# Lightweight convolution into a SiLU feed-forward layer: the third block's halo columns are copied by ScalarE instead of Pool

## The chip, the core and the metric

One NeuronCore of a Trainium2 chip runs the whole kernel. The metric is the device time of one execution in microseconds (us). The engines are named as in the profile: PE is TensorE's matmul, PEld its weight load, DVE is VectorE, ACT is ScalarE, POOL is GpSimd, and SP is SyncE, which only issues DMAs here. An engine works through its own queue in order; semaphores tie the queues together.

## What is computed

```python
w = softmax(weight, axis=-1)                    # (8 heads, 7 taps)
x_pad = concat([zeros(B, 6, D), x], axis=1)     # x is (8, 4096, 192), causal padding
out = einsum('hk,bskhg->bshg', w, windows of 7 of x_pad)   # depthwise, taps shared in a head
h = out.reshape(32768, 192) @ w_in              # (192, 2048)
y = (h / (1 + exp(-h))) @ w_out                 # SiLU, then (2048, 192)
```

Everything is float32 in and out. Row t of a sequence needs rows t-6 to t: each block of rows needs the last six rows of the block before it, its halo.

## The kernel before

The 32768 rows are worked in 32 blocks of `TT` = 1024 rows, numbered b = 0 to 31; four blocks make a sequence. The third block is b = 2. On chip a block lies transposed: channels on partitions, rows along the free axis, in two halves of 512 rows, the first on partitions 0 to 63 and the second on 64 to 127. The one tile `xt` holds this for the current block, with `pad` = 6 halo columns in front of the 512 in each of three channel groups k.

Making a block ready takes these steps, one block ahead of its matmuls:

- `load` brings rows from HBM into `nat` (L140), and `turn_in` transposes them on DVE into `xt` (L425).
- `halo_in` fills the halo columns. For the first half they come from a small tile, `tail`: the line L442 copies them on Pool, 64 partitions by 18 elements. For a block that starts a sequence, L440 writes zeros in their place. For the second half a DMA on SP takes them from the first half's last columns (L443). Then `tail_of` saves the block's own last six columns by a DMA into the next `tail` (L435).
- `conv` computes the seven taps: for b of 2 or more the first tap is a multiply on DVE (L454) and the others a multiply-add on DVE (L457). For b below 2 the first tap is on ScalarE (L452). The first tap reads the halo columns, so it waits for all of `halo_in`.
- `spread` copies the result into `dup` by DMAs on SP (L474), and `win` makes sums and differences of these on DVE (L491, L494).

The matmuls of a block follow a scheme with fewer products than the plain one. `product` (L579) and `plain` (L591) write PSUM; for each group, ScalarE copies a partial sum out of PSUM into a tile `u` (L615), DVE adds it to another partial sum (L611), and ScalarE applies SiLU (L627, L632). `out_slot` (L683) is the second layer, `merge` and `turn_out` bring its result together, and `store_out` (L772) writes it out by DMAs on SP.

The scheme needs weights that are combined beforehand. `combine` and `combine_out` do that on Pool, once, by some ninety additions and subtractions (L319, all through the helper `comb`), while the first block is worked in the plain way. The first block's second layer is `down_plain` (L702), which ends in three copies on ScalarE (L715).

From the second block on, the string `PLAN` gives the order: it lists tokens, and `step` turns each into instructions for block b, the block before it or the block after it. `ha.0` in the pass of block b is `halo_in(b + 1)`; so the third block's halo is filled in the pass of the second block, b = 1, which is also the first pass that runs by `PLAN`. In this pass, `ha.0` stands ahead of the first ScalarE token, `u5.0`.

Most instructions of PE, DVE and ScalarE are pinned (`pin`, and the wrappers `vec` and `act`): they keep the order in which the code issues them. The additions of `comb` and the copy L442 go straight to `nc.gpsimd` and are not pinned; the framework's scheduler places them in Pool's queue. In the built program, the copy for b = 2 stands second to last of this queue's preparatory work: the last addition of `combine_out` follows it.

Of the kernel before, what the change touches and what calls it, by code (L numbers as in the profile page):

```python
# [17 lines left out]
def kernel(  # L18
# [24 lines left out]
    nc = tc.nc  # L43
# [7 lines left out]
    R = 64  # L51
    NK = D // R
    grp = D // H
    pad = K - 1
# [60 lines left out]
    def pin(ins):  # L115
        return tc.keep_in_program_order(ins)
# [303 lines left out]
    tails = {}  # L420
# [11 lines left out]
    def tail_of(b):  # L432
        if (b + 1) * TT % S:
            tails[b + 1] = xpool.tile([R, NK, pad], F32, tag="tail", name="tail", bufs=2)
            nc.sync.dma_start(out=tails[b + 1], in_=xts[b][R:P, :, TB : TB + pad])  # L435

    def halo_in(b, _):
        xt = xts[b]
        if b * TT % S == 0:
            nc.gpsimd.memset(xt[0:R, :, 0:pad], 0.0)  # L440
        else:
            nc.gpsimd.tensor_copy(xt[0:R, :, 0:pad], tails.pop(b))  # L442
        nc.sync.dma_start(out=xt[R:P, :, 0:pad], in_=xt[0:R, :, TB : TB + pad])  # L443
        tail_of(b)

# [344 lines left out]
    def step(b, token):  # L790
# [13 lines left out]
        if name[0] == "P":  # L804
            product(b, digits[0], int(name[1:]))
        elif name == "L":
            plain(b, *digits)
        elif name == "SL":
            silu_plain(b, *digits)
        elif name[0] in "uXabS":  # L810
            sums_h(b, name, digits[0])
        elif name == "t":
            sum_g(b, *digits)
        elif name[0] == "D":
            i, (j, e) = int(name[1]), digits
            for half in range(2) if i == 3 and b == NB - 1 else (None,):
                out_slot(b, j, i, e, half)
        elif name[0] in "Mzyx":
            merge(b, name, *digits)
        elif name == "o":  # L820
            turn_out(b, *digits)
        elif name == "st":
            store_out(b, *digits)
        elif name == "ld":
            if b + 1 < NB:
                load(b + 1, digits)
        elif b + 1 < NB:
            {"i": turn_in, "ha": halo_in, "v": conv, "sp": spread, "w": win}[name](
                b + 1, *digits[: 1 + (name == "v")]
            )  # L830
# [212 lines left out]
```

## Time and profile before

| | us |
|---|---|
| median of 4 runs | 2418.73 |
| lowest to highest | 2418.28 to 2419.95 |
| profiled execution, its own time | 2418.76 |
| its span, first to last instruction | 2417.0 |
| PE busy | 2389.7 (99% of the span) |
| DVE busy | 2137.3 (88%) |
| ACT busy | 1149.1 (48%) |
| POOL busy | 115.3 (5%) |

The span leaves out 1.76 us around the first and last instruction. A line such as `ACT u L615 <- PE ps L579` in the view of waits says that ACT, about to write tile u at line 615, waited for PE's write of ps at line 579; the figures are the total, the number of waits and the longest. A line of the timeline has the start, the time taken (from the first start to the last end where several are merged), engine, line, operation, tiles, count, and in brackets the idle time before it with what ended that.

### The profile page before, as it was taken

The page shows a single profiled execution, that of the slowest core. Times are in us where ns is not written, and L with a number is a line of the kernel's source. Part 1 is how long each engine was busy: PE and PEld are TensorE (multiplying, and loading weights), DVE is VectorE, ACT ScalarE, POOL GpSimd, SP SyncE. Part 2 cuts the span into 40 slices and gives each one's busy share as a digit, 9 for nine tenths or more (in the row PEclk, how much of TensorE's full clock was granted, in tenths as well). Part 3 has the DMA queues.
Part 4 walks back from the last instruction along what each step waited for, and adds up shares of the span by engine and source line. Part 5 has one row for each costly group of instructions (what it writes and reads, how often), then busy time and mean ns, then how long its engine had stood idle before and what let it go on. Part 6 is the DMA issues. An engine that isn't in the chain of part 4 may idle for free.

```text
span 2417.0 us, 43592 instructions
## 1 busy us (share of the span) xinstructions
PE 2389.7 (99%) x17630; PEld 979.1 (41%) x17630; DVE 2137.3 (88%) x2967; ACT 1149.1 (48%) x2183; POOL 115.3 (5%) x169
## 2 busy tenths in 40 slices
PE   9789999999999999999999999999999999999998
PEld 4234443444433444434444334443344443344433
DVE  8689888999889898889998899988899988999876
ACT  4145444455444554444554445544445544455443
POOL 5900000000000000000000000000000000000000
PEclk9999999999999999999999999999999999999999
DMA  7411222221222212222212222122222122221111
GB/s 150 80 38 24 42 45 45 51 43 27 47 41 48 51 24 43 44 44 51 45 27 45 41 48 51 26 41 46 42 51 47 25 45 42 48 51 29 26 33 18
DMA packets 451242, 106.54 MB, mean 44 GB/s; under 512 B 423584, under 2 KB 428704, under 8 KB 451040
## 3 DMA queue, kind: packets, MB, share of 16 engines
q1 hardware_dynamic: 447392, 101.78, 23.1%
q8 instruction: 138, 2.26, 0.4%
q0 software_dynamic: 448, 1.58, 0.3%
q10 hardware_dynamic: 3200, 0.39, 0.1%
q14 instruction: 64, 0.52, 0.1%
HBM read 31.46 MB, written 25.17 MB: 23 GB/s over the span
## 4 chain that ended last, share of the span: by engine, by line
PE 94%; DVE 0%; ACT 0%; issue 0%; POOL 0%; ACTq 0%
PE ps L683 47%; PE ps L579 45%; PE ps L591 2%; DVE t L123 0%; DVE nat L457 0%; DVE cmb L123 0%; ACT u L123 0%; DVE g L611 0%; DVE nat L454 0%; DVE osb L123 0%; DVE ps L611 0%; DVE u L611 0%; ACT u L615 0%; POOL wo L319 0%; ACTq L871 0%
## 5 line engine op out<-in xcount | busy, mean ns | idle before, releaser
L579 PE MATMUL ps<-win,ws 64*128 64x512 f32 x1550 | 703.0, 609 | 18.5 <-DVE ps L611 17.8
L683 PE MATMUL ps<-g,wo 128*32 128x512 f32 x2976 | 708.7, 594 | 0.0
L579 PE MATMUL ps<-win,wr 64*128 64x512 f32 x1550 | 656.8, 609 | 0.7 <-ACT u L615 0.7
L615 ACT COPY u<-ps 128x512 f32<-128x512 f32 x775 | 451.1, 587 | 210.6 <-PE ps L579 196.6
L683 PE MATMUL ps<-t,wo 128*32 128x512 f32 (+2 forms) x4528 | 543.6, 446 | 0.0
L683 PE MATMUL ps<-t,wx 128*32 128x512 f32 x2976 | 491.7, 594 | 0.1
L627 ACT ACTIVATE g<-g 128x512 f32<-128x512 f32 x465 | 279.1, 628 | 438.7 <-DVE g L611 438.7
L457 DVE SCALAR_TENSOR_TENSOR nat<-xt,taps,nat 128x512 f32<-128x512 f32 x564 | 419.3, 748 | 7.8 <-ACT nat L452 3.8
L579 PE MATMUL ps<-dup,wr 64*128 64x512 f32 x868 | 411.1, 593 | 0.0
L123 DVE TENSOR_TENSOR t<-g 128x1024 f32<-128x1024 f32 x248 | 301.7, 1217 | 54.6 <-PE ps L683 53.7
L579 PE MATMUL ps<-dup,ws 64*128 64x512 f32 x682 | 345.8, 603 | 0.0
L123 DVE TENSOR_TENSOR t<-g,t 128x1024 f32<-128x1024 f32 x248 | 302.3, 1220 | 46.0 <-PE ps L683 44.9
L579 PEld LDWEIGHTS ps<-win,wr 64*128 64x128 f32 x1550 | 234.5, 186 | 234.1 <-issue 86.2
L611 DVE TENSOR_TENSOR g<-u,ps 128x512 f32<-128x512 f32 x465 | 313.7, 679 | 15.0 <-PE ps L579 14.2
L579 PEld LDWEIGHTS ps<-win,ws 64*128 64x128 f32 x1550 | 240.1, 186 | 177.9 <-DVE ps L611 69.0
L627 ACT ACTIVATE g<-ps 128x512 f32<-128x512 f32 x465 | 263.8, 596 | 56.5 <-PE ps L579 56.5
L683 PEld LDWEIGHTS ps<-t,wo 128*32 128x32 f32 x4528 | 179.1, 110 | 239.4 <-issue 228.6
L611 DVE TENSOR_TENSOR ps<-u,ps 128x512 f32<-128x512 f32 x310 | 214.3, 691 | 58.9 <-ACT u L615 26.3
L683 PE MATMUL ps<-g,wx 128*32 128x512 f32 x1488 | 246.8, 595 | 0.0
L683 PEld LDWEIGHTS ps<-t,wx 128*32 128x32 f32 x2976 | 115.5, 110 | 269.4 <-issue 261.0
L683 PEld LDWEIGHTS ps<-g,wo 128*32 128x32 f32 x2976 | 162.0, 110 | 135.4 <-issue 135.4
L742 ACT COPY cmb<-ps 96x512 f32<-96x512 f32 x30 | 17.5, 582 | 418.8 <-PE ps L683 418.8
(89 smaller groups left out, 1825.9 us busy)
## 6 DMA issues: line engine op xcount, KB each, us to landing
dup<-nat SPq DMA_DIRECT2D x345, 128.0 KB, 2.3
nat<-in_x_dram SPq DMA_DIRECT2D x382, 64.0 KB, 2.5
out_dram<-osb SPq DMA_DIRECT2D x376, 64.0 KB, 2.0
raw<-in_moe_w_out_dram SPq DMA_DIRECT2D x8, 384.0 KB, 4.1
raw<-in_moe_w_in_dram SPq DMA_DIRECT2D x12, 192.0 KB, 4.7
ws<-wr POOLq DMA_DIRECT2D x8, 192.0 KB, 3.5
raw<-in_moe_w_in_dram SPq DMA_DIRECT2D x6, 128.0 KB, 3.1
xt<-xt SPq DMA_DIRECT2D x31, 4.5 KB, 1.9
```

Of the source, the lines that this page charges most:

```text
L123: return lambda *args, **kw: pin(getattr(self.engine, name)(*args, **kw))
L457: nc.vector.scalar_tensor_tensor(out=dst, in0=src, scalar=tap, in1=dst, op0=ALU.mult, op1=ALU.add)
L579: nc.tensor.matmul(to, raw(g, *LEFT[e][r], e), rhs, start=first, stop=True, skip_group_check=True)
L591: nc.tensor.matmul(banks[PLAIN_BANKS[n and 1 + e]][:, cols], rows(wr[j] if own == e else ws[j], e)[:, a, k, :], rows(dups[b], e)[:, SLOT[e ...
L611: pin(nc.vector.tensor_tensor(out_, u, v, op=op))
L615: pin(nc.scalar.copy(us[b, g, o], t1))
L627: pin(nc.scalar.activation(h, src, AF.Silu))
L683: nc.tensor.matmul(accs[b][at][SQ * q : SQ * q + SQ, to], lhs[:, e, SQ * k : SQ * k + SQ], rhs[:, e, ts(q, TB // 4) if i == 5 else to], st ...
L742: pin(nc.scalar.copy(c[0], acc[0][0:n, :]))
```

## The change

For b = 2, and for that block alone, the copy of the halo columns goes to ScalarE and is pinned at the place where the code issues it. All other blocks keep the copy on Pool.

```diff
         if b * TT % S == 0:
             nc.gpsimd.memset(xt[0:R, :, 0:pad], 0.0)
         else:
-            nc.gpsimd.tensor_copy(xt[0:R, :, 0:pad], tails.pop(b))
+            head = xt[0:R, :, 0:pad]
+            if b == 2:
+                pin(nc.scalar.copy(head, tails.pop(b)))
+            else:
+                nc.gpsimd.tensor_copy(head, tails.pop(b))
         nc.sync.dma_start(out=xt[R:P, :, 0:pad], in_=xt[0:R, :, TB : TB + pad])
         tail_of(b)
```

In the built program ScalarE's queue has the new copy right behind the three copies of L715 and ahead of the first copy of L615. Pool's queue lacks it. The orders of PE, DVE and SP are the same as before. The waits of the new copy are those of the old one: the last multiply-add of block b = 1 on DVE, the DMA that filled `tail`, and ScalarE's own first taps of block b = 1.

## The prediction

> **What bounds the kernel now.** I began with the chain that ended last, by engine, and then asked for the waits of PE, because a chain that lies almost wholly on one engine can only shorten where that engine stood idle.
>
> ```profile
> PE 94%; DVE 0%; ACT 0%; issue 0%; POOL 0%; ACTq 0%
> ```
>
> ```profile
> engine line waited for: us in total, times, longest us
> PE ps L579 <- DVE ps L611: 17.8, 1, 17.8
> PE ps L579 <- ACT u L615: 0.7, 1, 0.7
> PE ps L579 <- POOL wr L319: 0.6, 1, 0.6
> ```
>
> The kernel runs at PE's pace and PE waits once in earnest, 17.8 us, for a DVE sum. The blocks behind it follow each other on PE without idle time. So the question is what held that one DVE sum. The timeline of DVE around it:
>
> ```profile
> 107.55 1.84 DVE L425 STREAM_TRANSPOSE xt<-nat 128x512 f32<-128x512 f32 x3
> 122.18 1.19 DVE L454 TENSOR_SCALAR nat<-xt,taps 128x512 f32<-128x512 f32 x2 [12.78 <-POOL xt L442]
> 123.40 2.99 DVE L457 SCALAR_TENSOR_TENSOR nat<-xt,taps,nat 128x512 f32<-128x512 f32 x4
> 126.30 0.69 DVE L611 TENSOR_TENSOR ps<-u,ps 128x512 f32<-128x512 f32 x1
> ```
>
> DVE works in order. The sum at 126.30 stands behind two first taps and four multiply-adds of the third block, and the first of these stood 12.78 us for the halo copy on Pool. The timeline of Pool says why the copy was late:
>
> ```profile
> 119.66 0.59 POOL L319 TENSOR_TENSOR wx<-wx,wo 128x192 f32<-128x192 f32 x1
> 120.33 0.59 POOL L319 TENSOR_TENSOR wx<-wo,wx 128x192 f32<-128x192 f32 x1
> 120.87 1.14 POOL L319 TENSOR_TENSOR wo<-wo 128x192 f32<-128x192 f32 x2
> 121.95 0.19 POOL L442 COPY xt<-tail 64x18 f32<-64x18 f32 x1
> 122.10 0.58 POOL L319 TENSOR_TENSOR wo<-wo 128x192 f32<-128x192 f32 x1
> ```
>
> Pool had no gap: the copy waited for no data, only for its turn behind the weight additions. The path to the stall is Pool's queue, then copy, taps, sum, and PE at 127.05.
>
> **What the change removes.** The copy leaves Pool's queue. Its conditions were met long before: the last multiply-add of block b = 1 ended at 97.88 (a run of 18 that starts at 81.75 and takes 16.13), and the DMA into `tail` was issued at 80.0, with 1.9 us to landing. ScalarE comes to it here:
>
> ```profile
> 102.07 0.59 ACT L715 COPY cmb<-ps 128x512 f32<-128x512 f32 x1 [0.27 <-PE ps L702]
> 103.11 0.59 ACT L615 COPY u<-ps 128x512 f32<-128x512 f32 x1 [0.46 <-PE ps L579]
> ```
>
> The last L715 copy ends at 102.66, and that is when the new copy can start. Its price on ScalarE has no row of its own. The nearest are ScalarE's 32x128 copies (L734, 256 ns mean) and the 128x1 activation at the start (203 ns); I take 0.25. It fits into the 0.46 us in which ScalarE waits for PE. If it did not, the `u` copies behind it would move, PE waits for those at 103.75, and each microsecond would cost one there; but PE then still runs into the stall, so up to several microseconds stay covered by it. Cost: nothing. Two table loads of 1.28 us, should the copy need them, would lie under the same cover.
>
> The Trainium skill, "TensorE: Matmul & The Clock Gate", in the section on the array's architectural detail, states that ScalarE's queue is strict first in, first out, so a waiting copy there would hold up every `u` copy and SiLU behind it. By that rule alone the move would be a danger; here nothing of its waits is left at 102.66, so it adds nothing to the sum.
>
> **What is late next.** DVE's first tap needs three things: the halo copy (now about 102.9), DVE's own transposes (ended 109.39), and the DMA L443 for the second half's halo, on SP:
>
> ```profile
> 106.46 6.34 SPq L772 DMA_DIRECT2D out_dram<-osb  x12
> 112.91 0.64 SPq L443 DMA_DIRECT2D xt<-xt  x1
> ```
>
> It stands behind the twelve stores of the first block, is issued at 112.91 and takes 1.9 us from issue to landing (the row of DMA issues for this stretch). Nothing ahead of it on SP depends on the copy, so it lands at 114.8, and the taps start at about 114.85 in place of 122.18: 7.33 us earlier. The new limit is this DMA, not the copy.
>
> **What the earlier start runs into.** From 109.4 to 122 DVE stood still and Pool had its inputs to itself. With taps from 114.85, both work. The trace shows what that costs on both sides: the 18 multiply-adds at 81.75, beside Pool, went at (16.13 - 1.0) / 17 = 0.89 us each, the four at 123.40, without it, at (126.30 - 123.40) / 4 = 0.725. And the two first taps:
>
> ```profile
> L454 DVE TENSOR_SCALAR nat<-xt,taps x2: 474/633/792, 122.2 to 122.9; 128x512 f32<-128x512 f32 x2
> ```
>
> The first, beside Pool's last addition, took 0.79 us and the second 0.47; from start to start the slow one held DVE for 0.72 and the fast one for 0.50. So before the sum: one more slow tap, 0.22, and four slow multiply-adds, 4 x (0.89 - 0.725) = 0.66; together 0.88 us. The sum itself reads PSUM and has no row beside Pool in this place; I leave it. It starts at 114.85 + (126.30 - 122.18) + 0.88 = 119.85, and PE follows 0.75 later, as before: 120.60 in place of 127.05. Gain 6.45 us. Without contention it would be 7.33; with all six instructions and the sum at the worst row's ratio, 0.79 / 0.47 = 1.68 times, 4.12 + 0.69 becomes 8.1 and the gain 4.1.
>
> Pool pays too: its additions take 0.45 alone and 0.79 beside DVE (64x128), so the 7.6 us of work left at 114.85 could last 7.6 x 0.79 / 0.45 = 13.3 us, to 128.2. What it makes then is weights. The first-layer ones are finished two microseconds after 114.85 before and, slowed, at about 118.2, ahead of PE's restart; the last ones are for L683, which PE starts 25 us after the restart (152.15 against 127.05). Cover is ample; if it were gone, each late microsecond would be one of PE's.
>
> **The clock.** PE stands still for 11.4 us (109.23 to 120.60) in place of 17.8. The granted clock in this stretch, by windows:
>
> ```profile
> 109.40:127.00 17.60, 0.00 (x0) 0.00 (x0) 4.72 (x8) 0.58 (x2) 12.20 (x26) 0.60 0.28 42
> 127.00:130.00 3.00, 2.96 (x10) 1.75 (x12) 2.24 (x4) 0.59 (x1) 0.00 (x0) 0.51 0.00 0
> 130.00:140.00 10.00, 10.00 (x52) 5.14 (x52) 6.83 (x12) 5.92 (x12) 0.00 (x0) 1.00 0.01 2
> ```
>
> The clock is the figure after POOL's. A mean of 0.60 over 17.6 us is 3.5 us at full and the rest at half speed, so it fell near 112.9, and it came back near 129.95, 2.9 us after the restart; those 2.9 us at half speed cost PE 1.45. With 11.4 us idle it still falls, so I take the same cost again, a difference of nothing. No row shows another restart; I bound it by -1.45 (back at once) and +1.45 (twice as long). The four runs, 1.67 us apart, leave room for that.
>
> The same page of the skill, Part 1, says that the clock is set by free-running windows of 3.4 us, so the slow stretch after a restart depends on where in a window it falls. By that rule an estimate of the stretch is anything up to two windows, 6.8 us, which costs at most (6.8 - 2.9) / 2 = 1.95 us more than before and 1.45 less at best; the trace's 2.9 agrees with it but shows one case.
>
> **The sum.** Behind the restart the work is the same and PE has no idle time in which the shift could be lost. The profiled execution's own time of 2418.76 becomes 2418.76 - 6.45 = 2412.3. The median, 2418.73, is 0.03 lower, so the same.
>
> **The rivals.**
> (a) As worked out, 2412.3; with the bounds on contention at none and on the clock at half their width, 2410.9 to 2413.8. Chance 0.83.
> (b) The halo DMA is late. It has become the limit, and its lines show landings from 1.8 up to 3.7 us. At 3.7 the gain is 6.45 - 1.8 = 4.65, and with 0.3 lost to the clock 4.35: 2414.4. For it: stores and loads share its queue. Against it: this very DMA took 1.9 in the same surroundings. Chance 0.10. The heavy contention above gives about the same time.
> (c) Nothing moves, because DVE was really held by something else that ended at 122.1: 2418.7. Pool's copy ended at 122.14 and DVE began at 122.18, and nothing else in sight ended there. Chance 0.04.
> (d) Slower: the copy holds up ScalarE's queue. Behind it stand three `u` copies that the DVE sum needs, 4.2 us from the first's start (103.11) to the third's end (107.32), and then 0.75 to PE. PE restarts later than before only if the copy ends after 127.05 - 0.75 - 4.2 = 122.1; from there each microsecond costs one. An end at 128 gives 2424.7. Against it are the conditions met by 97.88, 24 us of margin. Chance 0.03.
>
> **How the numbers follow.** A difference under 0.2%, 4.8 us, is about what a measurement of this kernel can't tell from none. Case (a) is faster throughout; of (b) the half with landings up to 3.5 us reaches 4.8. So faster has 0.83 + 0.05 = 0.88, same 0.05 + 0.04 = 0.09, slower 0.03. The range takes (a) and (b): 2410.9 to 2414.4.
>
> **What would show it.** In the changed profile: a ScalarE copy of 64x18 near 102.7; DVE's first tap near 114.9, held by the DMA L443's landing; multiply-adds of 0.8 to 0.9 us until Pool ends at 126 to 128; PE's one wait at about 11.4 us; and, from there on, each block 6 to 7 us earlier. I am wrong if the first tap starts later than 117, if PE waits for Pool's weights after the restart, or if a new idle stretch opens later on PE.

## The result, and the profile after

| | us |
|---|---|
| before, median of 60 runs | 2419.49 (2416.82 to 2422.24) |
| after, median of 40 runs | 2415.11 (2412.71 to 2416.55) |
| after against before, ratio | 0.9982, 95% interval 0.9978 to 0.9987 |
| forecast | 2412.3, range 2410.9 to 2414.4 |

The change makes the kernel faster by 4.4 us, 0.18%. The direction is as forecast, the size is not: 6.45 us were forecast, and the time lies above the range. The first four runs of before had a median 0.76 us lower than the sixty, so part of the miss is the base; the larger part is the gain.

The profiled execution has a span of 2414.2 us, against 2417.0. The lines of `kernel.py` behind the edit stand four further down: L442 is now L444 for the third block, L454 is L458, L457 is L461, L579 is L583, L611 (the sum on DVE) is L615, L615 (the `u` copy on ScalarE) is L619. The chain that ended last and the waits of PE, after:

```profile
PE 94%; DVE 3%; SPq 1%; DMA 1%; issue 0%; ACT 0%; ACTq 0%; DVEq 0%
```

```profile
engine line waited for: us in total, times, longest us
PE ps L583 <- DVE ps L615: 12.9, 1, 12.9
```

The one long wait is still there and still for the same sum; it went from 17.8 to 12.9 us, where 11.4 were forecast. ScalarE's queue shows the copy (start, time taken, then what it is):

```profile
102.10 0.20 ACT L444 COPY xt<-tail 64x18 f32<-64x18 f32 x1
102.66 0.59 ACT L619 COPY u<-ps 128x512 f32<-128x512 f32 x1 [0.35 <-PE ps L583]
```

It takes 0.20 us, and the `u` copy behind it still waits for PE. Then SP's queue and DVE's:

```profile
113.60 0.63 SPq L447 DMA_DIRECT2D xt<-xt  x1
```

```profile
108.25 1.85 DVE L425 STREAM_TRANSPOSE xt<-nat 128x512 f32<-128x512 f32 x3
115.60 1.24 DVE L458 TENSOR_SCALAR nat<-xt,taps 128x512 f32<-128x512 f32 x2 [5.51 <-DMA xt<-xt]
116.88 5.32 DVE L461 SCALAR_TENSOR_TENSOR nat<-xt,taps,nat 128x512 f32<-128x512 f32 x4
122.11 0.68 DVE L615 TENSOR_TENSOR ps<-u,ps 128x512 f32<-128x512 f32 x1
```

The first taps now wait for the halo DMA, as forecast. But the four multiply-adds take 5.32 us, where the kernel before needed 2.99 and 3.6 were forecast. One of them alone, from the rows of L461 in this stretch (shortest, median and longest in ns):

```profile
L461 DVE SCALAR_TENSOR_TENSOR nat<-xt,taps,nat x1: 2464/2464/2464, 117.7 to 117.7; 128x512 f32<-128x512 f32 x1
```

And what Pool did meanwhile (the profile before has 114 such additions and subtractions on Pool in all):

```profile
117.23 0.78 POOL L319 TENSOR_TENSOR ws<-wr,ws 64x128 f32<-64x128 f32 x1
117.97 0.58 POOL L319 TENSOR_TENSOR wx<-wo 128x192 f32<-128x192 f32 x1
118.52 0.58 POOL L319 TENSOR_TENSOR wo<-wo 128x192 f32<-128x192 f32 x1
119.06 0.58 POOL L319 TENSOR_TENSOR wx<-wx,wo 128x192 f32<-128x192 f32 x1
119.72 0.92 POOL L319 TENSOR_TENSOR wx<-wo,wx 128x192 f32<-128x192 f32 x1
```

Three additions follow each other every 0.55 us at the 0.58 us that Pool needs with DVE still. 3 x 0.55 = 1.64, and 2.464 - 0.823 (the shortest multiply-add in this stretch) = 1.64: the times are those of a multiply-add that did not advance during these three. The other five multiply-adds of the stretch took 0.82 to 1.14 us, and most of Pool's 128x192 additions beside them 0.92 to 1.04: there both were slowed and both went on. The last view is the clock, by windows (the figure after POOL's):

```profile
110.00:122.80 12.80, 0.00 (x0) 0.00 (x0) 7.19 (x9) 0.66 (x2) 11.72 (x22) 0.69 0.39 59
122.80:128.60 5.80, 5.75 (x20) 3.57 (x22) 3.20 (x4) 0.97 (x2) 3.06 (x4) 0.51 0.01 3
128.60:140.00 11.40, 11.40 (x54) 5.49 (x50) 8.32 (x13) 7.98 (x15) 0.00 (x0) 1.00 0.00 1
```

PE restarted at 122.85. A mean of 0.51 over the second window puts the return to full speed near 128.45, so PE ran at half speed for 5.6 us, against 2.9 before: 1.35 us more lost than in the first profile.

### The profile page after: what moved, and what is told of

Read it like the earlier page. It is cut to its first block, busy times and chain, and to the rows that moved or that the text cites. A ratio compares the mean times of both kernels' runs of the same rounds, so it can differ in the third digit from the quotient of the medians.

```text
span 2414.2 us, 43590 instructions
## 1 busy us (share of the span) xinstructions
PE 2390.9 (99%) x17630; PEld 982.8 (41%) x17630; DVE 2140.4 (89%) x2967; ACT 1149.1 (48%) x2184; POOL 116.4 (5%) x168
## 4 chain that ended last, share of the span: by engine, by line
PE 94%; DVE 3%; SPq 1%; DMA 1%; issue 0%; ACT 0%; ACTq 0%; DVEq 0%
PE ps L687 47%; PE ps L583 45%; PE ps L595 2%; DVE two L123 1%; DVE nat L461 1%; DVE mh L123 0%; SPq L140 0%; SPq L776 0%; DMA nat<-in_x_dram 0%; DMA raw<-in_moe_w_in_dram 0%; DMA xt<-xt 0%; SPq L235 0%; DVE win L495 0%; SPq L230 0%; DMA dup<-nat 0%
## 5 line engine op out<-in xcount | busy, mean ns | idle before, releaser
L583 PE MATMUL ps<-win,ws 64*128 64x512 f32 x1550 | 703.5, 610 | 13.6 <-DVE ps L615 12.9
L583 PE MATMUL ps<-win,wr 64*128 64x512 f32 x1550 | 656.7, 609 | 0.7 <-ACT u L619 0.7
L619 ACT COPY u<-ps 128x512 f32<-128x512 f32 x775 | 451.1, 587 | 207.4 <-PE ps L583 191.2
L461 DVE SCALAR_TENSOR_TENSOR nat<-xt,taps,nat 128x512 f32<-128x512 f32 x564 | 422.2, 753 | 7.8 <-ACT nat L456 3.8
L583 PE MATMUL ps<-dup,wr 64*128 64x512 f32 x868 | 411.7, 594 | 0.8 <-POOL wr L319 0.8
L583 PE MATMUL ps<-dup,ws 64*128 64x512 f32 x682 | 345.8, 603 | 0.0
L583 PEld LDWEIGHTS ps<-win,wr 64*128 64x128 f32 x1550 | 234.7, 186 | 234.5 <-issue 86.8
L615 DVE TENSOR_TENSOR g<-u,ps 128x512 f32<-128x512 f32 x465 | 313.7, 679 | 15.1 <-PE ps L583 14.2
L583 PEld LDWEIGHTS ps<-win,ws 64*128 64x128 f32 x1550 | 240.3, 186 | 173.1 <-DVE ps L615 64.1
L615 DVE TENSOR_TENSOR ps<-u,ps 128x512 f32<-128x512 f32 x310 | 214.3, 691 | 58.3 <-ACT u L619 26.3
```

The source lines that it names most:

```text
L461: nc.vector.scalar_tensor_tensor(out=dst, in0=src, scalar=tap, in1=dst, op0=ALU.mult, op1=ALU.add)
L583: nc.tensor.matmul(to, raw(g, *LEFT[e][r], e), rhs, start=first, stop=True, skip_group_check=True)
L615: pin(nc.vector.tensor_tensor(out_, u, v, op=op))
L619: pin(nc.scalar.copy(us[b, g, o], t1))
```

## The experiments

Theory A: the missing gain was lost to Pool, which shut DVE out. Theory B: something else slowed DVE. Theory C: the clock took it. Each run is set against the kernel before on the same chip, which had medians of 2419.3 to 2419.5 us.

**The changed kernel again** (no edit).

> The changed kernel once more, unaltered, for a second profile. Known: 2415.1 us against 2419.5 before; in its first profile the four multiply-adds ahead of the sum took 5.2 us, one of them 2.46, where 3.6 were forecast. Theory A (Pool's unpaused additions of 128x192 shut DVE out of its inputs): it comes again, one of the four takes about 1.6 us more than 0.82, and PE's wait is 12 to 13 us. Theory B (a chance of that one execution): no multiply-add over 1.1 us, the four take 3.6, and PE's wait is 11.4.

Measured: 2414.51 us, ratio 0.9978 (0.9970 to 0.9987).

```profile
115.11 1.25 DVE L458 TENSOR_SCALAR nat<-xt,taps 128x512 f32<-128x512 f32 x2 [5.50 <-DMA xt<-xt]
116.40 5.31 DVE L461 SCALAR_TENSOR_TENSOR nat<-xt,taps,nat 128x512 f32<-128x512 f32 x4
121.63 0.68 DVE L615 TENSOR_TENSOR ps<-u,ps 128x512 f32<-128x512 f32 x1
```

The 5.3 us come again, with a longest multiply-add of 2464 ns once more. It is no chance of one execution: the same three additions meet a multiply-add again.

**Additions held back**, with the copy on ScalarE (`late`) and, with the same edit, on Pool (`late_before`):

```diff
+        def comb(out, u, v, op):
+            pool.tensor_tensor(out, u, v, op=op)
...
-        if (b, token) == (1, "ha.0"):
+        if (b, token) == (1, "v.12"):
             assert not any(t[0] == "D" for c, t in did if c == 1)
+            pool.tensor_copy(wx[0][:, 0, 0, 0:1], nats[2][:, 1, 0, 0:1])
             for j in range(NJ):
                 combine_out(j)
```

The first lines stand in `combine_out`; `pool` is the pinned wrapper of Pool. The one-column copy reads what the last tap ahead of the sum has written, so the additions behind it wait for this tap.

> The changed kernel, with the additions of combine_out held back on Pool until the last tap ahead of the sum is done (a one-column copy on Pool reads this tap's result, and the additions stand behind it). Theory A (contention with Pool is what the gain lost): the six taps before the sum take 4.1 us as in the kernel before, the sum starts at about 119.7 and PE's wait falls from 12.9 to about 10.5; 2412.7 us, 2.4 less than the changed kernel. Theory B (DVE was slowed by something else, the loads and stores of that stretch or ScalarE): the taps still take 6.5, PE's wait stays near 12.9, 2415.1.

> The kernel before, halo copy on Pool, with the same additions held back. Theory A (the copy was late only for its place in Pool's queue behind these additions, and the halo DMA of the second half is the next limit): the copy comes before 114, the first tap waits for the DMA at about 115, and the time is that of the run with the copy on ScalarE and the additions held back, 2412.7 within 0.7. Rival (the move to ScalarE matters in itself): it stays clearly above that, up to 2419.5.

Measured: `late` 2411.86 us, ratio 0.9967 (0.9954 to 0.9979); `late_before` 2411.28, ratio 0.9965 (0.9953 to 0.9978). DVE in `late`:

```profile
115.52 0.88 DVE L461 TENSOR_SCALAR nat<-xt,taps 128x512 f32<-128x512 f32 x2 [6.43 <-DMA xt<-xt]
116.44 2.99 DVE L464 SCALAR_TENSOR_TENSOR nat<-xt,taps,nat 128x512 f32<-128x512 f32 x4
119.34 0.69 DVE L618 TENSOR_TENSOR ps<-u,ps 128x512 f32<-128x512 f32 x1
```

With Pool still, the four take 2.99 again and the sum comes 3.82 us after the first tap, in place of 6.51. The loads and stores still run in this stretch (the issue of the twelve stores even took 7.26 us in place of 6.34), so theory B falls. Holding the additions back is worth 2414.51 - 2411.86 = 2.65 us, close to the 2.7 by which the taps became shorter; all five runs of `late` lie below all forty of the changed kernel. Both times came out below the 2412.7 expected. PE's wait was 12.3, not the 10.5 expected, though it restarted at 120.1: it had also come to the wait earlier. Pool and the first tap in `late_before`:

```profile
112.55 0.19 POOL L445 COPY xt<-tail 64x18 f32<-64x18 f32 x1
118.84 0.18 POOL L123 COPY wx<-nat 128x1 f32<-128x1 f32 x1 [6.09 <-DVE nat L460]
```

```profile
114.87 0.88 DVE L457 TENSOR_SCALAR nat<-xt,taps 128x512 f32<-128x512 f32 x2 [5.50 <-DMA xt<-xt]
```

The copy on Pool is in time as soon as the additions no longer stand ahead of it, and the DMA is the limit there too. So it was the place in the queue, not the engine: with the additions held back, the kernel gains 8.3 us with the copy on Pool and 7.7 with it on ScalarE, against 5.0 for the changed kernel on the same chip. Part of this gain is the contention that the same edit takes away.

**Additions in the code's order** (`inorder`): the changed kernel with the additions of `combine_out` pinned as above, but neither held back nor moved to another token.

> The changed kernel with the additions of combine_out pinned on Pool in the order of the code, but not held back: all sixteen then run after the last addition of combine, and nearly each waits for the one ahead of it. Theory A1 (DVE is shut out whole only while Pool runs several additions without a pause, 1.6 us for the three in the changed kernel): no tap takes more than 1.4 us, the six taps take 5.0 to 5.5, the sum starts near 120.5, 2413.5. Theory A2 (any 128x192 additions shut DVE out, whatever their order): the taps take 6.5 or more and the time is 2415 or above.

Measured: 2413.14 us, ratio 0.9973 (0.9962 to 0.9983). The multiply-adds of the stretch:

```profile
L464 DVE SCALAR_TENSOR_TENSOR nat<-xt,taps,nat x6: 958/961/1073, 116.3 to 121.8; 128x512 f32<-128x512 f32 x6
```

Pool's 128x192 additions run beside all of them, and none is shut out: 0.96 to 1.07 us each. The first tap to the sum takes 5.18 us, inside the 5.0 to 5.5 of A1, so A2 falls. But A1, that a run of additions without a pause shuts DVE out, does not follow. Pool's rows here:

```profile
116.09 0.65 POOL L123 TENSOR_TENSOR wx<-wo,wx 128x192 f32<-128x192 f32 x1
116.70 1.03 POOL L123 TENSOR_TENSOR wo<-wo 128x192 f32<-128x192 f32 x1
117.69 1.03 POOL L123 TENSOR_TENSOR wx<-wo 128x192 f32<-128x192 f32 x1
```

These three follow each other without a pause too, and both engines went on. The order of the additions decides whether the standstill comes; what in the order does it is not shown.

**PE kept busy through the stall** (`heat`):

```diff
+        if (b, token) == (1, "P1.0"):
+            for _ in range(12):
+                pin(
+                    nc.tensor.matmul(
+                        banks[6],
+                        zeros,
+                        zeros.unsqueeze(1).to_broadcast([P, 4, P]),
+                        start=True,
+                        stop=True,
+                        skip_group_check=True,
+                    )
+                )
         if name[0] == "P":
             product(b, digits[0], int(name[1:]))
```

> The changed kernel, with 12 idle matmuls of 128x512 on zeros in front of the product that waits for the sum, into a bank that nothing else uses then. By the products' rate they take about 10.3 of the 12.9 us. Theory C (part of the loss is the clock, at half speed for 2.9 us after the restart before and 5.7 in the profile after): the granted clock stays at 1.00, the restart is at full speed, and the time falls by 1.4 to 2.9 us, to about 2412.9, with less spread. Rival (the clock's share is only in the profiled execution): 2415.1.

Measured: 2413.13 us, ratio 0.9972 (0.9961 to 0.9983), 1.4 less than the changed kernel beside it. But it is no clean test: PE still waited 2.6 us at the end, and the clock did not stay up as expected: it fell at 123.0, just after the restart at 122.46, and was low for 3.4 us. The taps, too, met Pool differently: one first tap took 1.81 us, beside the same three additions at 0.58 us each, a second case of the standstill. PE restarted as late as in the second profile of the changed kernel (122.37), where the slow stretch lasted 6.0 us; (6.0 - 3.4) / 2 = 1.3 us fits the 1.4. So the clock costs something, of the order of a microsecond; one profile does not measure how much.

**The kernel before again** (`before_again`, no edit).

> The kernel before once more, unaltered, for a second profile: how long the clock stays at half speed after PE's restart. If the 2.9 us of the first profile were short by chance, this one shows more, like the 4.7 to 6.1 us of the runs so far; if a longer stall makes a shorter slow stretch, it shows about 2.9 again. PE's wait 17.8, 2419.5 us within 1.5.

Measured: one time, 2419.07 us; PE's wait 17.8 again. The windows of the first profile, here:

```profile
127.00:130.00 3.00, 2.84 (x10) 1.64 (x12) 2.25 (x5) 0.58 (x1) 0.00 (x0) 0.50 0.00 0
130.00:140.00 10.00, 10.00 (x48) 5.29 (x46) 5.76 (x10) 4.73 (x10) 0.00 (x0) 0.89 0.01 2
```

A mean of 0.89 over 10 us is 2.2 us at half speed: the clock came back near 132.2, 5.1 us after the restart at 127.16. The 2.9 us that the forecast was built on were at the short end. The clock by windows of 0.1 us and, from the chain, the start of the first long stretch of second-layer matmuls, in two profiles of each kernel:

| | before | before again | after | after again |
|---|---|---|---|---|
| clock falls | 112.89 | 111.76 | 114.79 | 111.34 |
| PE restarts | 127.05 | 127.16 | 122.85 | 122.37 |
| clock is back | 129.96 | 132.24 | 128.45 | 128.40 |
| half speed after the restart | 2.9 | 5.1 | 5.6 | 6.0 |
| second layer starts | 164.17 | 165.35 | 161.31 | 161.04 |

Against `before_again`, where the slow stretch is nearly as long, the changed kernel is 4.0 and 4.3 us ahead, close to the 4.4 of the medians, and its PE restarts 4.3 and 4.8 us earlier. So the clock explains why the first pair of profiles is only 2.8 us apart. That it takes nothing from the medians is likely, but two profiles of each kernel do not show it.

From fall to return the clock was at half speed for 17.07, 20.48, 13.66 and 17.06 us: 5, 6, 4 and 5 steps of 3.41, to 0.02 us. A restart paid the rest of the step into which it fell and, in three of the four, the next one whole; where the steps lie differs between executions of one program.

**Halo ahead of the stores** (`early_lb`, on top of `late_before`): `turn_out` and `store_out` of the first block are issued at `ha.0`, behind `halo_in`.

```diff
+        if (b, token) == (1, "ha.0"):
+            out_first()
...
-    for k in range(NK):
-        turn_out(0, k)
-        store_out(0, k)
+    def out_first():
+        for k in range(NK):
+            turn_out(0, k)
+            store_out(0, k)
```

> The kernel before with the additions held back and the first block's output transposes and stores issued behind the third block's halo. Theory (the halo DMA behind the twelve stores is the limit once the copy is early): DVE transposes the third block at about 105.7, the DMA is issued near 108 and lands near 110, the taps start at 110 to 110.5 or, if Pool's copy comes at 112.5, at 112.7; PE's wait falls from 11.7 to 7 to 9.5; 2407 to 2409.5 us. Rival (something else holds DVE): 2411.3 as without the move.

Measured: 2410.14 us, ratio 0.9961 (0.9948 to 0.9973), a little above the expected range.

```profile
107.51 0.63 SPq L446 DMA_DIRECT2D xt<-xt  x1
```

```profile
112.66 0.88 DVE L457 TENSOR_SCALAR nat<-xt,taps 128x512 f32<-128x512 f32 x2 [3.44 <-POOL xt L445]
```

The DMA goes out 5.4 us earlier than in `late_before`, and the limit is Pool's copy again, which stands behind the additions of `combine`. PE restarts at 117.23 in place of 119.43, but its slow stretch lasted 5.8 us here, against 5.3.

**Sums ahead of the taps** (`spread`, then `spread_a`, and `spread_b` with the copy on Pool):

```diff
+    put_off = []
     for b in range(1, NB + 2):
-        for s in plan:
+        for n, s in enumerate(plan):
             for t in s:
-                step(b, t)
+                if b == 1 and t[:2] == "v." and (n < 53 or put_off):
+                    put_off.append(t)
+                else:
+                    step(b, t)
+            if put_off and n > 52 and n % 3 == 2:
+                step(b, put_off.pop(0))
```

The first of the three lacked `(n < 53 or put_off)`. In it the last tap of a channel group comes behind the DMAs that spread the group's result, so it leaves this tap out of what the matmuls read and does not compute the layer; it serves for its time alone.

> The changed kernel, where the third block's taps are put behind the first four sums and then given one by one to every third slot of the plan in this pass. Theory (PE's stall is nothing but the taps standing ahead of the sums in DVE's queue): PE's long wait is gone, at most 3 us are left at that place, and the time falls by up to 11 us under the changed kernel, to 2404; what DVE then has too much in the rest of the pass can give back some us as short waits of PE, so 2404 to 2409. Rival (DVE lacks the time in this pass, and PE waits as long, only later): 2413 to 2417.

> The changed kernel with the taps put behind the sums as in the run before this one, where the last tap of a channel group came behind the DMAs that spread it; here it comes ahead of them again. Theory (PE's stall was the order of taps and sums in DVE's queue, and DVE has the time for the taps later in the pass): 2404.3 within 0.8, no wait of PE over 1 us behind 104. Rival (the earlier run was that fast for its misplaced tap): above 2406.

> The same order of taps and sums with the halo copy on Pool, as in the kernel before. Theory (the copy stays behind Pool's additions until about 122, and the first tap, which DVE reaches at about 116, waits for it): DVE stands for some 5 to 6 us at the first tap, PE for 4 to 6, and the time is 2408 to 2410; the move to ScalarE is then worth 4 to 6 us in this order too. Rival (the sums ahead of the taps leave enough slack to hide the late copy): 2404 to 2405, and the copy's place no longer matters.

Measured: `spread` 2404.35 us, ratio 0.9934 (0.9922 to 0.9947); `spread_a` 2404.65, ratio 0.9937 (0.9925 to 0.9950); `spread_b` 2410.06, ratio 0.9960 (0.9946 to 0.9973). PE's longest wait for DVE in `spread_a`, and DVE's wait for Pool in `spread_b`:

```profile
PE ps L583 <- DVE ps L615: 2.6, 1, 2.6
```

```profile
DVE nat L454 <- POOL xt L442: 6.1, 1, 6.1
```

The sums depend on nothing that the taps make. Issued first, they free PE at 110.4, the clock is at half speed for 3.4 us only (111.1 to 114.5), and DVE finds time for the taps later. `spread_a` beats both kernels, by 14.6 us over before; its one wait of 2.6 us was expected under 1. In `spread_b` the late copy costs 2410.06 - 2404.65 = 5.4 us: in this order too, getting it out from behind the additions is needed.

## Why the prediction was right, and where not

- **The stall and its chain** (Pool's queue, copy, taps, sum, PE): right. `late_before` and `spread_a` each break it at another link, and PE's wait follows. The blocks behind it came 2.9 to 4.3 us earlier, by the profiles compared, where 6 to 7 were forecast.
- **The copy on ScalarE**: right, 0.20 us at 102.10, forecast 0.25 near 102.7. It moved nothing.
- **The halo DMA as next limit**: right. Its landing took 1.9 us again. The first tap started at 115.60 and 115.11 in place of 114.85, because DVE's work ahead of it, and with it the DMA's issue, lay 0.7 and 0.2 us later in these executions.
- **"What the earlier start runs into"**: the step that failed, by its size. Contention was named as the price of the earlier start, but charged by the mean of 18 multiply-adds beside other additions, 0.88 us in all. From the first tap to the sum 6.51 and 6.52 us passed, against 5.0 forecast and 4.12 before: contention cost 2.4, of which 1.64 is one multiply-add that stood still for three additions. The rate came from a stretch whose 18 multiply-adds took at most 1.08 us each, and was carried to one in which Pool's additions come in another order. The 2.4 in place of 0.88 is 1.5 us of the 2.1 by which the gain fell short (6.45 against 4.4). The later first tap, named above, took another 0.75 and 0.26 us in the two profiles; the two together leave 4.2 and 4.7 us of the 6.45, which is how much earlier PE restarted in them than in the first profile before. `late` puts the contention at 2.65 us of time.
- **The range** does not follow from its sentence: contention at none and half the clock's width give 2410.7 to 2413.0, while 2410.9 and 2413.8 are 2412.3 with the clock's full 1.45 on either side. And it left out what the text itself had worked out: the heavy bound on contention, a gain of 4.1, gives 2414.7, above the range's end. The measured 4.4 lies close to it. Rival (b), a late DMA, came to a similar time for a wrong reason.
- **The clock**: "the same cost again" fits the medians, and is wrong between the first two profiles, since 2.9 us was a short sample. The bound of +1.45 was about met: 1.35 in one profile of the changed kernel, 1.55 in the other. The Trainium skill ("TensorE: Matmul & The Clock Gate", Part 1) states a free-running window of about 3.4 us. The steps of 3.41 us in these profiles agree with it, and the estimate of up to two windows, 6.8 us, covers the 2.9 to 6.0 seen after the restart; it would have been the better guide to the spread.
- **Pool's lateness**: right. Its additions ended at 125.9 and 125.4 (126 to 128 forecast), and PE waited for none of them after the restart.
- **The chance of 0.88** for faster by over 0.2%, 4.8 us, stood on this step above all: with contention at its measured price the forecast gain is 7.33 - 2.39 = 4.9, on that line, and the measured 4.4 lies below it. That a change under 0.2% can't be told from none was wrong: the interval of the ratio is 0.0005 to either side.

## What to carry to other kernels

When a wait goes, ask what now runs at the same time that ran in turns before, and price that overlap by the worst row as well as by the mean. Here the bound by the worst row, a gain of 4.1 us, lay next to the measured 4.4, though no row of the profile before showed a standstill. A helper's late result can be a matter of the queue it stands in, as here: look first at the order ahead of it, and at what is queued behind the waiter without needing it, before moving work to another engine. Here the order of two groups on DVE alone gained 9.2 us (`spread_b`), about twice the move; both together gained 14.6.

## What the runs showed of the hardware

Pool and DVE slow each other unevenly. A 128x512 multiply-add took 0.75 us alone, 0.82 to 1.14 beside most additions, and 2.46 across three that each took Pool's undisturbed 0.58; a first tap went from 0.48 to 1.81 across the same three in `heat`. Pool's 64x128 addition went from 0.45 to 0.79. The Trainium skill, "GPSIMD Engine Reference", section 8, Key points, says that GpSimd shares its SBUF interfaces with VectorE and contends with instructions that have two SBUF inputs; the runs agree.

PE's clock fell after an idle stretch of 2.6 us in `heat`. In `spread` it fell at 105.0 although PE had been busy for 2.1 of the 3.4 us before and idle for 0.7 at a time at most. The half-speed stretch after a restart ranged from 2.9 to 6.0 us in four profiles of the two kernels, while the whole time at half speed around this stall, idle part included, was a whole number of steps of 3.41 us in each profile of this case, from one step in `heat` to six in `before_again`.
